# A gated sum of a long convolution and a GLU: one table for the last stage of the inverse transform, fewer warming matmuls, two down products in another bank, and new queue orders

## The chip, the core and the metric

The kernel runs on one core of a Trainium2 chip. The core has five engines, each with its own instruction queue that is worked off in order: TensorE (PE, with its weight loads shown apart as PEld), VectorE (DVE), ScalarE (ACT), GpSimd (POOL) and SyncE (SP), which only issues DMAs. The metric is the device time of one execution in microseconds (us), lower is better. Comparisons are of medians of several runs on one chip.

## The reference, cut to what matters

```python
x = A_u                                            # (1, 2048, 448), f32
g = sigmoid((x * gate_w).sum(-1, keepdims=True))   # one gate per position
# branch a: a diagonal state-space convolution over the 2048 positions
A = -exp(log_A_real) + 1j * A_imag                 # (448, 256)
C = (C_real + 1j * C_imag) * dt[:, None]
K = 2 * einsum("dn,dnl->dl", C, exp((A * dt[:, None])[:, :, None] * pos)).real
y = irfft(rfft(K, 4096) * rfft(u.T, 4096), 4096)[:, :2048]
a = y.T + u * D_skip
# branch b: GLU with a sigmoid gate, 448 -> 1792 -> 448
b = (sigmoid(x @ w_gate) * (x @ w_up)) @ w_down
out = g * a + (1 - g) * b
```

Both branches read the same x (an input B_x is drawn but not used).

## The kernel before, in words

**Four pieces of work.** (1) *Prologue* (`step_sizes`, `params`, lines 998 to 1176): from the small parameters come the step sizes, phases and powers of the convolution kernel, mostly on VectorE and ScalarE. `step_sizes` also holds the warming: `WAKE` matmuls of a tile of ones into a PSUM tile that nobody reads (L1030), first in TensorE's queue. `params` broadcasts the step sizes over the partitions with one matmul (L1072) whose input is two scaled identity blocks made on VectorE (L1069).

(2) *Kernel generation* (`kgen`, 28 chunks of 16 channels): GpSimd makes powers (`powers`), TensorE multiplies positions by phases (L1223) and subtracts the whole turns (L1232), ScalarE rounds and takes sines (L1227 to L1245; L1229 makes the whole turns that L1232 needs), VectorE forms outer products (L1252) and multiplies them in (L1266, L1269), TensorE contracts (L1281, after the second half chunk's L1269), and ScalarE copies the result to `ke` (L1302). After chunk 13 and chunk 27 a half of the channels is complete: VectorE adds the skip weights to `ke` (L1306) and the half goes to DRAM.

(3) *Transforms* (class `Chain`): a transform of 4096 points as two stages of table matmuls, for u (two halves of the channels) and for K (two halves, called chains 0 and 1 here). For each K half: `stage1` (L812), a transposition, `product` with the spectrum of u (L845, L879, L889), a transposition, and `back`: the last stage of the inverse, 16 blocks j, each two matmuls (L926) with a quarter q = j // 4 of the table `t1t`, then one VectorE instruction (L930) that scales by the gate and adds to the output tile.

(4) *GLU* (`glu_groups`): for each half H of the positions and each group of the 14 feature blocks, `glu_up` (L1414 to L1419, rounded f32 in three products, gate L1398, L1400 or L1403 to L1406) and `glu_down` (L1433 in plain f32 or L1435 to L1437 in three rounded products), with L1445 or L1452 taking the result from PSUM into the output tile `ob`.

**Memory.** PSUM tiles come from pools by tag: `gu` has two, `dn` one, `fps` of pool fups two, of pool fkps three. In `back` each chain loads the four quarters of `t1t` itself, 256 KB each, into a tile with tag `ft` (chain 1, two buffers) or `ftx` (chain 0, which has moved to pool fk by then; one buffer), so a load waits until the tile before it has been used.

**What sets the order.** Instructions are first only recorded (`Plan.op`). The table `PLACE` gives each of them its place in its engine's queue, by engine, tag and priority; it was written by a search outside this file. `Plan.order` merges the queues with a cost model of the engines and emits them. The places within an engine are fixed by the table: an instruction that has to wait holds up all that is behind it on its engine, SyncE's DMA issues too.

The two lines that name the numbers that change:

```python
SX = {'ft': 1, 'ua': 2, 'fps': 2}
WAKE = 24
```

Of the kernel before, what the change touches and what calls it, by code (L numbers as in the profile page):

```python
# [20 lines left out]
HD = 224  # L21
# [7 lines left out]
    ('Act', 'aci', 10): (15, 36,),  # L29
    ('Act', 'aci', 19): (64, 87,),  # L30
    ('Act', 'acr', 10): (13, 34, 43,),
    ('Act', 'acr', 19): (60, 85, 94,),
# [26 lines left out]
    ('Act', 'dots', 1): (27,),  # L59
    ('Act', 'dots', 2): (50,),  # L60
    ('Act', 'dots', 16): (80, 82,),
# [284 lines left out]
SX = {'ft': 1, 'ua': 2, 'fps': 2}  # L346
# [352 lines left out]
WAKE = 24  # L699
# [879 lines left out]
```

## Time and profile before

| | |
|---|---|
| median of 3 runs | 691.46 us (689.62 to 694.54) |
| span of the profiled execution | 688.4 us |
| its own time | not given apart; the median is 3.1 us above the span, the lowest run 1.2 |
| TensorE busy | 673.8 us |
| VectorE busy | 602.0 us |
| ScalarE busy | 510.0 us |
| DMA | 123.84 MB, 180 GB/s on average |

The page gives the busy time of each engine, the span in 40 slices of 17.2 us, the chain of work that ended last, and groups of instructions by line with the tiles that they write and read. Names like `dn_gps` are tag and pool. An idle time is shown with what ended it, `<-` and the instruction. The starts of matmuls tell more than their durations, since matmuls overlap.

### The profile page before, as it was taken

Reading aid. Unit: us, or ns where it says so; the run is one execution under the profiler, and the core shown is the slowest. Engines: PE = TensorE matmul, PEld = TensorE weight load, DVE = VectorE, ACT = ScalarE, POOL = GpSimd, SP = SyncE. Lnnn points to the kernel's source line nnn. Section 1 sums busy time; section 2 is a strip of 40 time slices with the busy share of each in tenths; the row PEclk is TensorE's granted clock in tenths of the full one; section 3 lists DMA queues with packets and bytes.
Section 4 is the critical chain, followed back from the end, with each engine's and each line's share of the span. In section 5 each row is a group of like instructions: output and inputs, shape, how many; then the busy total and the mean of one; then the engine's idle time right before and its main releaser. Section 6 shows DMA issues by size and latency. Waiting matters only on the chain.

```text
span 688.4 us, 16283 instructions
## 1 busy us (share of the span) xinstructions
PE 673.8 (98%) x6588; PEld 483.1 (70%) x6588; DVE 602.0 (87%) x699; ACT 510.0 (74%) x928; POOL 274.9 (40%) x280
## 2 busy tenths in 40 slices
PE   9999999999999999999899999999999999999996
PEld 8776667877886687775556676788888766556873
DVE  5999999999999999989999789999973489577976
ACT  5677699899999999999999999999941352233110
POOL 0315268865447656675663845667000000000000
PEclk9999999999999999999999999999999999999999
DMA  9769342656896787737966974457948973979866
GB/s 252 180 177 246 87 108 70 153 138 237 186 182 157 177 215 178 225 112 177 193 171 144 233 199 90 140 168 184 180 100 202 271 235 124 312 246 241 166 179 165
DMA packets 97474, 123.84 MB, mean 180 GB/s; under 512 B 31096, under 2 KB 80568, under 8 KB 96376
## 3 DMA queue, kind: packets, MB, share of 16 engines
q1 hardware_dynamic: 97400, 122.81, 69.8%
q8 instruction: 52, 0.85, 0.5%
q14 instruction: 22, 0.18, 0.1%
HBM read 79.20 MB, written 43.58 MB: 178 GB/s over the span
## 4 chain that ended last, share of the span: by engine, by line
PE 73%; ACT 10%; DVE 8%; DMA 5%; issue 2%; SPq 1%; ACTq 0%; DVEq 0%
PE gu_gps L1414 9%; PE gu_gps L1415 8%; PE gu_gps L1416 8%; PE kp_egp L1281 6%; PE dn_gps L1433 5%; PE dn_gps L1435 4%; PE tp_egp L1232 4%; PE dn_gps L1436 4%; PE dn_gps L1437 4%; PE tp_egp L1223 4%; PE fps_fups L812 3%; PE gu_gps L1418 3%; PE gu_gps L1419 3%; PE fps_fups L845 2%; PE fps_fups L889 2%
## 5 line engine op out<-in xcount | busy, mean ns | idle before, releaser
L1414 PE MATMUL gu_gps<-xs_glu,wh_glu 128*128 128x512 f32 x336 | 144.5, 430 | 1.4 <-DVE hl_glu L1400 0.9
L1416 PE MATMUL gu_gps<-xs_glu,wl_glu 128*128 128x512 f32 x336 | 131.8, 392 | 0.0
L1415 PE MATMUL gu_gps<-xs_glu,wh_glu 128*128 128x512 f32 x336 | 131.7, 392 | 0.0
L1269 DVE TENSOR_TENSOR cs_eg<-cs_eg,es_eg 128x2048 f32<-128x2048 f32 x56 | 129.2, 2307 | 1.4
L1252 DVE TENSOR_TENSOR es_eg<-tb_eg 128x1024 f32<-128x1024 f32 x112 | 110.5, 1003 | 3.0 <-POOL tb_eg L1216 0.9
L1213 POOL TENSOR_TENSOR tb_eg<-tb_eg 128x96 f32<-128x96 f32 (+2 forms) x84 | 107.5, 1284 | 5.9
L1216 POOL TENSOR_TENSOR tb_eg<-tb_eg,bs_eg 128x32 f32<-128x32 f32 x84 | 83.9, 1001 | 5.8
L1414 PEld LDWEIGHTS gu_gps<-xs_glu,wh_glu 128*128 128x128 f32 x336 | 63.2, 188 | 30.2 <-issue 13.0
L1398 ACT ACTIVATE sg_glu<-gu_gps 128x512 f32<-128x512 f32 x56 | 33.7, 603 | 58.3 <-PE gu_gps L1419 58.3
L1266 DVE TENSOR_TENSOR cs_eg<-cs_eg,es_eg 128x1024 f32<-128x1024 f32 x56 | 70.5, 1260 | 7.2 <-ACT cs_eg L1245 6.0
L1229 ACT ACTIVATE nn_eg<-cs_eg 128x512 fp32r<-128x512 f32 x112 | 71.7, 640 | 4.5 <-PE tp_egp L1232 2.9
L1415 PEld LDWEIGHTS gu_gps<-xs_glu,wh_glu 128*128 128x128 f32 x336 | 63.3, 188 | 15.4 <-issue 4.8
L1416 PEld LDWEIGHTS gu_gps<-xs_glu,wl_glu 128*128 128x128 f32 x336 | 63.1, 188 | 14.5
L1452 DVE SCALAR_TENSOR_TENSOR ob_glu<-dn_gps,og,ob_glu 128x448 f32<-128x448 f32 x72 | 48.7, 676 | 25.1 <-PE dn_gps L1437 24.1
L1234 ACT ACTIVATE cs_eg<-tp_egp 128x512 f32<-128x512 f32 x112 | 66.5, 605 | 4.1 <-PE tp_egp L1232 3.6
L1227 ACT ACTIVATE cs_eg<-tp_egp 128x512 f32<-128x512 f32 x112 | 67.9, 607 | 1.6 <-PE kp_egp L1281 0.6
L1235 ACT ACTIVATE cs_eg<-tp_egp 128x512 f32<-128x512 f32 x112 | 67.3, 606 | 1.6 <-PE tp_egp L1232 1.4
L1245 ACT ACTIVATE cs_eg<-cs_eg,half_pi 128x1024 f32<-128x1024 f32 x56 | 65.2, 1165 | 0.4
L1281 PEld LDWEIGHTS kp_egp<-cs_eg 128*32 128x32 f32 x3584 | 51.5, 110 | 11.7 <-issue 6.3
L1281 PE MATMUL kp_egp<-cs_eg 128*32 128x64 f32 x3584 | 56.3, 220 | 0.5 <-issue 0.4
L1203 POOL MEMSET tb_eg<- 128x96 f32 x28 | 7.8, 285 | 116.4 <-DVE es_eg L1252 105.5
L1232 PE MATMUL tp_egp<-nn_eg,idn 128*128 128x512 f32 x112 | 49.7, 444 | 3.9 <-ACT nn_eg L1229 3.4
(161 smaller groups left out, 1326.2 us busy)
## 6 DMA issues: line engine op xcount, KB each, us to landing
shf<-fx_fu SPq DMA_DIRECT2D x16, 896.0 KB
fx_fu<-shf SPq DMA_DIRECT2D x16, 896.0 KB
us<-fx_fu SPq DMA_DIRECT2D x16, 896.0 KB
xr_glu<-in_w_dram SPq DMA_DIRECT2D x46, 256.0 KB
uax_fk<-us SPq DMA_DIRECT2D x16, 448.0 KB
ua_fk<-us SPq DMA_DIRECT2D x16, 448.0 KB
xr_glu<-in_w_dram SPq DMA_DIRECT2D x17, 224.0 KB
gt_pre<-in_u_dram SPq DMA_DIRECT2D x8, 448.0 KB
```

Of the source, the lines that this page charges most:

```text
L1213: pool(96 * m, lambda n=n, m=m: G.tensor_mul(g3(n + 1, m), g3(1, m), g3(n, 1).to_broadcast([128, 32, 3, m])))
L1216: pool(32, lambda e=e: G.tensor_mul(t(e + 1), t(e), b(3)))
L1227: op("Act", c_act(512, True), lambda: S.activation(cs[:, 1, ds, 32:96], block(tp), AF.Copy, bias=MAGIC), [tp], [(cs, ("s", i))], prio)
L1229: op("Act", c_act(512), lambda: S.activation(block(nn), cs[:, 1, ds, 32:96], AF.Copy, scale=-1.0, bias=MAGIC), [(cs, ("s", i))], [nn], prio)
L1232: op("PE", c_mm(532), lambda: T.matmul(tp.real, idn.real, nn.real, start=False, stop=True, skip_group_check=True), [nn, idn], [tp], prio)
L1252: V.tensor_mul(o.rearrange("p d (i k) -> p d i k", k=ny), x.unsqueeze(3).to_broadcast([128, 16, nx, ny]), y.unsqueeze(2).to_broadcast([128 ...
L1266: op("DVE", c_dve(1024), lambda: V.tensor_mul(cs[:, :, :, 0:32], cs[:, ::-1, :, 63:31:-1], es[:, :, 0:32].unsqueeze(1).to_broadcast([128, ...
L1269: op("DVE", c_dve(2048), lambda: V.tensor_mul(cs[:, :, :, 32:96], cs[:, :, :, 32:96], es[:, :, 32:96].unsqueeze(1).to_broadcast([128, 2, 1 ...
L1281: T.matmul(kp[32 * j:32 * j + 32, q], cs[:, z, 4 * j + q, 64:96], cs[:, z, 4 * j + q, 0:64], start=cs is parts[0] and z == 0 and q == 0, s ...
L1414: T.matmul(p.real, wh[:, k, cs], x[:, k], start=(k == 0), stop=False)
L1415: T.matmul(p.real, wh[:, k, cs], x[:, 4 + k], start=False, stop=False)
L1416: T.matmul(p.real, wl[:, k, cs], x[:, k], start=False, stop=False)
```

## The change

- `back` takes its table from one tile `t1` of all four quarters (8 KB in each partition, pool fk), loaded once by whichever chain asks first, quarter by quarter; both chains read it. The tags `ftx` and the last four uses of `ft` in chain 1 are gone. Eight loads become four.
- `WAKE` is 14 instead of 24.
- In the last GLU group of the second half, the down products of j = 5 and j = 7 use a `gu` tile of PSUM in place of the one `dn` tile.
- `PLACE` is a new table for all five engines. It has the same instructions apart from these.

The diff, without the table:

```diff
-SX = {'ft': 1, 'ua': 2, 'fps': 2}
+SX = {'ua': 2, 'fps': 2}
...
-WAKE = 24
+WAKE = 14
...
             hs = slice(self.h * HD, (self.h + 1) * HD)
-            tb = self.tile("ft", (128, TN, 128))
-            dma(lambda: tb.v("p l c -> p (l c)"), lambda: t1t[:, 512 * q:512 * q + 512], 128 * 2048,
-                [], [tb], prio)
+            tb = back_table(q, prio)
             for i in range(4 * q, 4 * q + 4, 2):
                 self.back_pair(i, tb, hs)
...
-                    T.matmul(p[64 * i:64 * i + 64, :HD], tb[:, l // 2, 64 * (l % 2):64 * (l % 2) + 64], x[:, 2 * j + i],
+                    T.matmul(p[64 * i:64 * i + 64, :HD], tb[:, j // 4, l // 2, 64 * (l % 2):64 * (l % 2) + 64], x[:, 2 * j + i],
                              start=True, stop=True)
             op("PE", c_mm4(HD, 2, COLS), f,
-               [tb, (x, j), *([] if self.on_dve else [(x, ("t", i)) for i in range(4)])], [p], self.prio)
+               [(tb, j // 4), (x, j), *([] if self.on_dve else [(x, ("t", i)) for i in range(4)])], [p], self.prio)
...
-    xs, ob = {}, {}
+    def back_table(q, prio):
+
+        if "t1" not in tables:
+            tables["t1"] = fk.tile("t1", 1, (128, 4, TN, 128))
+        t1 = tables["t1"]
+        if q not in tables:
+            tables[q] = True
+            dma(lambda: t1[:, q].rearrange("p l c -> p (l c)"), lambda: t1t[:, 512 * q:512 * q + 512], 128 * 2048,
+                [], [(t1, q)], prio)
+        return t1
+
+    xs, ob, tables = {}, {}, {}
...
     def glu_down(H, fs, j, hs, first, pe, prio):
-        p = gps.tile("dn", 1, (128, 512))
+        end = H == 1 and fs == FGS[1][-1] and j in (5, 7)
+        p = gps.tile("gu", GUB, (128, 512)) if end else gps.tile("dn", 1, (128, 512))
```

Of the table, three entries in full, the places of the broadcast L1072 (first number) with its two followers, of L1306, and of the loads of the last-stage table (old: the last four of the first line and the second line; the first four of it belong to `stage1`):

```diff
-    ('PE', 'fps', 10): (20, 56, 57,),
+    ('PE', 'fps', 10): (14, 55, 56,),
-    ('DVE', 'ke', 20): (348, 514,),
+    ('DVE', 'ke', 20): (350, 517,),
-    ('SP', 'ft', 41): (261, 272, 280, 284, 289, 292, 337, 351,),
-    ('SP', 'ftx', 40): (276, 333, 345, 354,),
+    ('SP', 'ft', 41): (266, 278, 284, 287,),
+    ('SP', 't1', 40): (264, 295, 277, 281,),
```

What these places mean where the prediction uses them, read out of the two tables:

```
VectorE near L1306 of the first half
  old: L1266, L1269 (chunk 13), L1306, L1252, L1345, L1252, L1266, L1452, L1400 (hl), L1269 (chunk 14)
  new: L1266, L1269 (chunk 13), L1452, L1252, L1400 (hl), L1306, L1252, xs, xs, L1452, L1266, L1269 (chunk 14)
TensorE at the start, matmuls ahead of L1072 and after the warming: old 53, new 36
TensorE work between L1223 and L1232 of a turn, shortest three of 112: old 0.2, 0.9, 1.0 us; new 1.4 us and up
TensorE, inverse blocks (L926) in a row, in the order of the runs:
  old 8, 6, 10, 2, 2, 2, 2      new 12, 6, 4, 3, 3, 3, 1
TensorE, the last eight: old  dn j4, L926, L926, dn j5, L926, L926, dn j6, dn j7
                         new  dn j4, dn j5, L926, L926, L926, dn j6, L926, dn j7
TensorE, groups of plain f32 products after the warming: old 72, new 69
TensorE, other changes of the array's shape: old 172, new 174
```

More of the change, by code (lines that the diff above doesn't have):

```diff
@@ L28 @@
 PLACE = {
[L29 to L32, printed above, removed]
[26 rows of a table removed]
[L59 to L61 removed]
[18 rows of a table removed]
[L80 to L82 removed]
[12 rows of a table removed]
[L95 removed]
[13 rows of a table removed]
+    ('Act', 'aci', 10): (14, 40,),
+    ('Act', 'aci', 19): (65, 94,),
+    ('Act', 'acr', 10): (15, 39, 49,),
+    ('Act', 'acr', 19): (63, 91, 101,),
[26 rows of a table added]
+    ('Act', 'dots', 1): (28,),
+    ('Act', 'dots', 2): (45,),
+    ('Act', 'dots', 16): (67, 83,),
[18 rows of a table added]
+    ('Act', 'idn', 10): (12,),
+    ('Act', 'junk', 10): (29, 60,),
+    ('Act', 'junk', 19): (77, 81, 132,),
[12 rows of a table added]
+    ('Act', 'pos_sb', 10): (36, 52,),
[13 rows of a table added]
     ('Act', 'wh', 0): (1, 4,),
     ('Act', 'wh', 1): (6, 7,),
[4 rows of a table removed]
[4 rows of a table added]
     ('Act', 'xs', 0): (0, 2, 3, 5,),
[2 rows of a table removed]
[L118 to L121 removed]
[15 rows of a table removed]
[L137 to L138 removed]
[14 rows of a table removed]
[L153 removed]
[24 rows of a table removed]
[L178 to L180 removed]
[6 rows of a table removed]
[L187 removed]
[6 rows of a table removed]
[L194 removed]
[71 rows of a table removed]
[2 rows of a table added]
+    ('DVE', 'aci', 10): (45,),
+    ('DVE', 'aci', 19): (122,),
+    ('DVE', 'acr', 10): (89,),
+    ('DVE', 'acr', 19): (152,),
[15 rows of a table added]
+    ('DVE', 'dtp', 10): (30,),
+    ('DVE', 'dtv', 10): (27,),
[14 rows of a table added]
+    ('DVE', 'half_pi', 0): (9,),
[24 rows of a table added]
+    ('DVE', 'ones', 10): (1,),
+    ('DVE', 'p', 10): (18, 20, 21, 22, 23, 25, 26,),
+    ('DVE', 'phs', 20): (2,),
[6 rows of a table added]
+    ('DVE', 'skip', 20): (0,),
[6 rows of a table added]
+    ('DVE', 'uax', 40): (539, 534, 546, 547, 556, 557, 570, 571, 578, 575, 585, 586, 590, 591, 595, 596, 624, 623,
[71 rows of a table added]
     ('Pool', 'bsx1', 10): (5, 11,),
[3 rows of a table removed]
[3 rows of a table added]
         56, 57, 58, 59, 60, 61, 62, 63, 64, 65, 66, 67, 68, 69, 70, 71, 72, 73, 74, 75, 76, 77, 78, 79, 80, 81, 82,
```

16 lines of the change are left out of this document (removed), and 530 rows, old and new, of the table PLACE.

## The prediction

> **What bounds the kernel now.** I read the page first: span, engines, slices, chain.
>
> ```profile
> span 688.4 us, 16283 instructions
> PE 673.8 (98%) x6588; PEld 483.1 (70%) x6588; DVE 602.0 (87%) x699; ACT 510.0 (74%) x928; POOL 274.9 (40%) x280
> ...
> DVE  5999999999999999989999789999973489577976
> ...
> PE 73%; ACT 10%; DVE 8%; DMA 5%; issue 2%; SPq 1%; ACTq 0%; DVEq 0%
> ```
>
> TensorE is busy for 98% of the span and carries 73% of the chain; VectorE is nearly as full until 500 us, while the convolution kernel is generated. A saving must be less work on TensorE or less idling there, and the idling is only 688.4 - 673.8 = 14.6 us. The waits of TensorE, and its busy time in some windows, say where.
>
> ```profile
> PE tp_egp L1232 <- ACT nn_eg L1229: 3.4, 7, 0.9
> ...
> PE dn_gps L1435 <- DVE ob_glu L1452: 0.8, 1, 0.8
> PE fps_fups L926 <- DMA ftx_fk<-in_t1t_dram: 0.6, 1, 0.6
> ```
>
> ```profile
> 684.00:689.00 5.00, 0.00 (x0) 0.73 0.44 104
> 310.00:350.00 40.00, 35.64 (x486) 1.00 0.87 172
> ```
>
> The columns of a window are its length, the busy time with the instructions, granted clock, DMA share and GB/s. TensorE idles 4.4 us between 310 and 350, from before 684 to the end, and 1.1 us at the start (the row of L1030 below). The code change touches the start and the waits of 0.6 and 0.8; only the new queue orders can touch the 4.4.
>
> A run's time is the span and what lies around it: the median of the three runs, 691.46, is 3.1 above this span, the lowest, 689.62, is 1.2 above. I work out differences for the profiled execution and put them on the median. The three runs differ by 0.7%, so less than about 1%, 6.9 us, can't be told from no change.
>
> **The start: 14 warming matmuls instead of 24.**
>
> ```profile
> L1030 PE MATMUL fps_fups<-ones_pro 112*128 112x128 f32 x48 | 8.5, 362 | 1.1 <-DVE half_pi L1497 1.1
> ```
>
> ```profile
> 2.05:3.05 1.00, 1.00 (x7) 1.00 0.94 307
> ...
> 7.50:8.50 1.00, 1.00 (x12) 1.00 0.99 355
> ```
>
> ```profile
> 6.54 0.69 DVE L1345 TENSOR_TENSOR xs_glu<-xr_pre,xs_glu 128x512 fp32r<-128x512 f32 x1 [0.51 <-ACT xs_glu L1341]
> ...
> 9.29 0.48 PE L1414 MATMUL gu_gps<-xs_glu,wh_glu 128*128 128x512 f32 x1
> ...
> 9.55 0.42 DVE L1347 TENSOR_TENSOR xs_glu<-xr_pre,xs_glu 128x256 fp32r<-128x256 f32 x1
> ...
> 10.46 0.69 DVE L1381 TENSOR_TENSOR wl_glu<-xr_pre,wh_glu 128x512 fp32r<-128x512 f32 x1
> ...
> 11.07 0.17 DVE L984 TENSOR_SCALAR xr_pro<-x_pro 112x4 f32<-112x4 f32 x1
> ...
> 11.27 0.17 DVE L984 TENSOR_SCALAR x_pro<-x_pro 112x4 f32<-112x4 f32 x1
> ...
> 20.22 0.27 DVE L1069 TENSOR_SCALAR rt_pro<-idn,dtv_pro 112x112 f32<-112x112 f32 x1
> ...
> 21.41 0.54 PE L1072 MATMUL fps_fups<-rt_pro,ones_pro 112*128 112x224 f32 x2
> ```
>
> A matmul of L1030 is two records. A window counts every record that overlaps it, so 7 records of about 0.4 us in 1 us are 5 starts per us. Fourteen matmuls, all in this slow part, take 28 / 5 = 5.6 us and end near 6.9. The first real matmuls need the L1345 that ends at 7.2, so TensorE starts them 2.0 us earlier. It can't keep that. After nine matmuls it needs the second part of x, which the L1347/L1348 pair from 9.55 to 10.46 makes; the new VectorE order puts a small step (0.2, from 11.07 to 11.27) and a one-column memset (0.1) in front of the pair, so 10.76. The old queue runs 53 matmuls from 9.29 to 21.41, 0.229 each, and starts the tenth at 11.35. Gained so far: 0.6.
>
> Then the new queue gives it back. L1072, which broadcasts the step sizes, now comes after 36 matmuls, not 53, so TensorE asks for it at 10.76 + 27 x 0.229 = 16.9. Its input is the second L1069. By the new order VectorE has from 9.55 until that is done two pairs of L1347/L1348 (0.91), four steps of 512 columns (0.61, from 10.46 to 11.07), twenty small ones (0.20) and the memset: 1.82 + 2.44 + 4.0 + 0.1 = 8.4, so 17.9. TensorE waits 1.0 us, and the 17 matmuls that used to come first stand behind: they end at 17.9 + 0.22 + 3.9 = 22.0, where the old queue is at 21.6. I take +0.4. Without that wait it is -0.6; with the input as late as now, at 20.5, it is +3.0.
>
> The granted clock is given as 1.00 in both windows above, yet the starts go from 5 to some 9 per us (12 records of about 0.3 us). The Trainium skill ("TensorE: Matmul & The Clock Gate", Part 1) says that the array runs at half rate until a free-running window of about 3.4 us has been busy, and again after an idle one. The slow part here, over 5 us, agrees. By that rule shortening the warming could leave real matmuls in the slow part; that is rival 4.
>
> **The end: the table and the bank.**
>
> ```profile
> 672.81 0.55 SPq L712 DMA_DIRECT2D ftx_fk<-in_t1t_dram  x1
> ...
> 675.31 5.15 SPq L712 DMA_DIRECT2D out_dram<-ob_glu  x8
> ...
> 676.83 0.98 PE L926 MATMUL fps_fups<-fx_fu,ftx_fk 128*64 128x224 f32 x8 [0.57 <-DMA ftx_fk<-in_t1t_dram]
> ...
> 681.17 4.44 SPq L712 DMA_DIRECT2D out_dram<-ob_glu  x7
> ...
> 682.78 0.47 PE L1435 MATMUL dn_gps<-vh_glu,hh_glu 128*128 128x448 f32 x1 [0.78 <-DVE ob_glu L1452]
> ...
> 683.68 0.69 DVE L1452 SCALAR_TENSOR_TENSOR ob_glu<-dn_gps,og,ob_glu 128x448 f32<-128x448 f32 x1 [0.96 <-PE dn_gps L1437]
> ```
>
> Eight loads of table quarters become four, all placed in SyncE's queue in the product stage. Of the old eight, three were there too, so that stage gets one issue more (0.55, hidden by SyncE's own waits; without that cover the input load behind it is 0.55 later), and the last 35 us lose five. The wait of 0.57 goes, since no quarter's buffer has to come free. The last down product no longer waits 0.78 for VectorE to empty the one dn bank. Together -1.35.
>
> What is late next? VectorE and the stores. Seven stores follow each other without a gap, 0.63 each, and the last two come right behind the last L1452, which ends at 684.37. Moved 1.35 forward they would meet a queue that is still busy, but two table loads (0.55 and about the same) leave that queue, which covers most of it. VectorE is nearer:
>
> ```profile
> L930 DVE SCALAR_TENSOR_TENSOR ua_fk<-fps_fkps,gs,ua_fk 128x224 f32<-128x224 f32 x8 | 3.6, 444 | 0.1
> ```
>
> ```profile
> 653.64 0.76 PE fps_fkps L926 x8
> ```
>
> (The second row is of the chain: eight records are two blocks, 0.38 each.) The new TensorE order starts with twelve inverse blocks in a row where there were eight, with five PSUM tiles between TensorE and VectorE, and VectorE needs 0.44 for each and has a vl step of 0.64 among them. That order makes TensorE wait about 12 x 0.06 = 0.7. So -0.65 in all; the ends are 0 and -1.35.
>
> **The middle: the orders.**
>
> ```profile
> 302.51 2.29 DVE L1269 TENSOR_TENSOR cs_eg<-cs_eg,es_eg 128x2048 f32<-128x2048 f32 x1
> 307.80 0.22 DVE L1306 TENSOR_TENSOR ke_eg<-ke_eg,skip 128x56 f32<-128x56 f32 x1 [2.99 <-ACT ke_eg L1302]
> 307.94 1.22 DVE L1252 TENSOR_TENSOR es_eg<-tb_eg 128x1024 f32<-128x1024 f32 x1
> 309.07 0.68 DVE L1345 TENSOR_TENSOR xs_glu<-xr_glu,xs_glu 128x512 fp32r<-128x512 f32 x1
> ...
> 312.00 0.67 DVE L1400 SCALAR_TENSOR_TENSOR hl_glu<-sg_glu,gu_gps 128x512 f32<-128x512 f32 x1
> 312.60 2.28 DVE L1269 TENSOR_TENSOR cs_eg<-cs_eg,es_eg 128x2048 f32<-128x2048 f32 x1
> ```
>
> At the end of the first half L1306 needs the contraction that itself needs the L1269 just before it, so VectorE stands for 2.99 us. The new order puts an L1452, an L1252 and an L1400 between the two: 0.6 + 1.13 + 0.6 = 2.3 us of work that VectorE has to do anyway. And VectorE is what the next 40 us wait for:
>
> ```profile
> 330.00:340.00 10.00, 7.76 (x146) 4.76 (x145) 9.86 (x8) 9.04 (x17) 7.83 (x7) 1.00 1.16 191
> ```
>
> ```profile
> 331.14 0.50 PE L1232 MATMUL tp_egp<-nn_eg,idn 128*128 128x512 f32 x1 [0.89 <-ACT nn_eg L1229]
> ...
> 339.28 0.50 PE L1232 MATMUL tp_egp<-nn_eg,idn 128*128 128x512 f32 x1 [0.78 <-ACT nn_eg L1229]
> ```
>
> (The first row: TensorE, its weight loads, VectorE, ScalarE, GpSimd.) The two waits of L1232 lie where the old order has only 0.2 to 1.0 us of other TensorE work between L1223 and L1232 of a turn (chunk 16); in the new order the shortest such distance is 1.4. These waits and VectorE's 2.3 lie in the same 4.4 us and can't be added. I take -3.0, nearer to the 4.4 than to the 0 that it is if ScalarE, 90% busy in the row above, sets the pace.
>
> ```profile
> 28.14 0.74 PE L1418 MATMUL gu_gps<-xs_glu,wh_glu 128*128 128x512 f32 x1
> 28.72 0.40 PE L1419 MATMUL gu_gps<-xs_glu,wl_glu 128*128 128x512 f32 x1
> ```
>
> The first rounded matmul after a plain f32 group takes 0.58 to the next one, not 0.23. The old order has 72 such groups, the new 69: -1.05. Other changes of the array's shape go from 172 to 174: +0 to +0.7, at the same price. I take -0.7. All other work is the same instructions in nearly the same places; I give it 0, with 2 us either way.
>
> **Sum.** +0.4 - 0.65 - 3.0 - 0.7 = -3.95, so 691.46 - 3.95 = 687.5.
>
> **Rivals.** 1. The gains are hidden: ScalarE paces the middle, VectorE and the stores the end. For it speaks ScalarE's 9.04 and VectorE's 9.86 of 10 us above. 691.46 + 0.4 - 0.7 = 691.2.
>
> 2. All of it comes: -4.4, -1.35, -0.6 and -1.05 are -7.4, 684.1. For it: the waits are plain in the rows. Against: something is always late next in a kernel that is this full.
>
> 3. Slower: ScalarE's queue holds the turns. Between L1227 and L1229 of a turn the new order has on average 0.37 more foreign ScalarE instructions than the old.
>
> ```profile
> L1229 ACT ACTIVATE nn_eg<-cs_eg 128x512 fp32r<-128x512 f32 x112 | 71.7, 640 | 4.5 <-PE tp_egp L1232 2.9
> ```
>
> At 0.64 that is 0.24 us per turn. On the 28 turns whose matmuls stand less than 2.5 us of TensorE work apart it becomes a TensorE wait of 6.6 us in all, and the gain of the middle is lost: 691.46 + 0.4 - 0.65 - 0.7 + 6.6 = 697.1. It decides where ScalarE is already late when L1227 is ready. Against it: the shortest distances grow.
>
> 4. The clock. TensorE idles some 1.4 us before 10.8 and 1.0 before 17.9. If that brings the slow rate back for as long as it lasted at the start, 5.6 us, 5/9 of the work is done in that time and the rest is late: 5.6 x 4/9 = +2.5, so 690.0. For it: the start is slow for that long at the same shown clock of 1.00. Against it: no stretch after the start shows the slow rate, but none before 310 idles as much either. The Trainium skill's page named above asks for a whole idle window before the rate falls, more than either gap; by that rule rival 4 doesn't come.
>
> **How the numbers follow.** The forecast has 0.46, rival 1 0.23, rival 2 0.18, rival 3 0.08, rival 4 0.05. The range leaves out most of rival 3 and the better half of rival 2: 683.0 to 694.0; the upper end is rival 1 with the late input at the start (3.0 instead of 0.4). The forecast's own range is 685 to 690. Faster by over 1% (under 684.5): two thirds of rival 2 and a tenth of the forecast, 0.18 with rounding up. Slower by over 1% (over 698.4): a third of rival 3 and what I haven't thought of, 0.06. Within: 0.76.
>
> **What would show it.** In the profile after: L1030 with 28 records ending before 7.3 and a wait of about 1 us at L1072 near 17 (right) or none (-0.6); L1306's first wait under 1 us and TensorE busy for over 38 of the 40 us from 310 (right), or VectorE's idle time moved elsewhere and TensorE's as before (rival 1); no wait for a table and none at the last down product; L1232's waits under 2 us in all, or over 6 (rival 3). I'm wrong if the time is under 683 without these, or if a new wait of several us stands in TensorE's list.

## The result, and the profile after

The changed kernel takes 688.62 us (median of 20 runs, 684.96 to 693.69) beside 692.16 us of the kernel before (20 runs, 689.62 to 695.45) on the same chip: a ratio of 0.9945, 95% interval 0.9924 to 0.9965, so 2.4 to 5.3 us less. On the 691.46 us of the prediction that is 687.7, where 687.5 was forecast. The sum was right. Its terms were not all right, and one cause that can move the time by more than any of them, late code for TensorE, was not in it.

The profiled execution took 684.96 us. The span, the engines, VectorE's slices and the chain of waits of its page:

```profile
span 683.0 us, 16235 instructions
...
PE 669.7 (98%) x6568; PEld 480.6 (70%) x6568; DVE 603.7 (88%) x699; ACT 509.7 (75%) x928; POOL 269.2 (39%) x280
...
DVE  7998999999899999999998999999974379667976
...
PE 82%; DVE 10%; ACT 3%; DMA 2%; issue 2%; SPq 1%; DVEq 0%
```

TensorE now carries 82% of the chain where it carried 73%; ScalarE's share fell from 10% to 3%. TensorE's busy time fell by 4.1 us and its idle time, 683.0 - 669.7 = 13.3 us, by 1.3. Line numbers from about 1039 on are nine or ten higher than before (L1315 is L1306, L1241 is L1232, L1462 is L1452).

The list of TensorE's waits (total, times, longest):

```profile
PE dn_gps L1443 <- DVE ob_glu L1462: 1.3, 2, 0.8
PE tp_egp L1241 <- ACT nn_eg L1238: 1.2, 1, 1.2
...
PE dn_gps L1445 <- DVE ob_glu L1462: 1.0, 1, 1.0
...
PE gu_gps L1423 <- DVE hh_glu L1409: 0.6, 1, 0.6
PE dn_gps L1443 <- DMA vh_glu<-in_w_dram: 0.5, 1, 0.5
PE fps_fups L1081 <- DVE rt_pro L1078: 0.4, 1, 0.4
```

The 3.4 us of L1232 are 1.2, and neither the wait for the table (0.6) nor that of the last down product (0.8) is in the list any more. The 1.0 of L1445 is another wait for the one dn bank, at 659.9, in the stretch of the inverse: VectorE empties the bank late there, after it has stood 0.86 us for a load (L928 at 658.45). Most of what is new stands in the head of the kernel: the timeline of TensorE there.

```profile
6.81 0.48 PE L1423 MATMUL gu_gps<-xs_glu,wh_glu 128*128 128x512 f32 x1
...
16.09 0.65 PE L1081 MATMUL fps_fups<-rt_pro,ones_pro 112*128 112x224 f32 x2 [0.41 <-DVE rt_pro L1078]
...
29.32 1.02 PE L1443 MATMUL dn_gps<-vh_glu,hl_glu 128*128 128x448 f32 x2 [0.45 <-DMA vh_glu<-in_w_dram]
...
30.95 0.50 PE L1423 MATMUL gu_gps<-xs_glu,wh_glu 128*128 128x512 f32 x1 [0.61 <-DVE hh_glu L1409]
...
34.11 1.02 PE L1443 MATMUL dn_gps<-vh_glu,hh_glu 128*128 128x448 f32 x2 [1.05 <-ACT ob_glu L1455]
```

The first real matmul is 2.5 us earlier than before (9.29), the broadcast of the step sizes 5.3 us earlier (21.41). Then three waits of 2.1 us in all follow within 5 us.

The end of the first half on VectorE, and TensorE's window behind it:

```profile
302.44 2.35 DVE L1278 TENSOR_TENSOR cs_eg<-cs_eg,es_eg 128x2048 f32<-128x2048 f32 x1
304.70 0.67 DVE L1462 SCALAR_TENSOR_TENSOR ob_glu<-dn_gps,og,ob_glu 128x448 f32<-128x448 f32 x1
305.30 1.21 DVE L1261 TENSOR_TENSOR es_eg<-tb_eg 128x1024 f32<-128x1024 f32 x1
306.43 0.67 DVE L1409 SCALAR_TENSOR_TENSOR hl_glu<-sg_glu,gu_gps 128x512 f32<-128x512 f32 x1
307.86 0.22 DVE L1315 TENSOR_TENSOR ke_eg<-ke_eg,skip 128x56 f32<-128x56 f32 x1 [0.75 <-ACT ke_eg L1311]
```

```profile
310.00:350.00 40.00, 37.85 (x506) 24.42 (x506) 39.40 (x36) 37.94 (x69) 28.11 (x27) 1.00 0.91 186
```

The wait of 2.99 is 0.75, and TensorE is busy 37.85 of the 40 us instead of 35.64, with 20 more matmuls.

To see where the time went in this and the other runs, each span is cut at five instructions: the first matmul of the contraction (L1281) of chunks 0, 13, 20 and 27, and of the first inverse block (L926). The kernels of the experiments are explained below; all numbers are us from one profile each.

| kernel | to chunk 0 | 0 to 13 | 13 to 20 | 20 to 27 | to inverse | to end | span |
|---|---|---|---|---|---|---|---|
| before | 114.9 | 190.0 | 97.8 | 102.0 | 146.4 | 37.2 | 688.4 |
| before, L1306 later | 113.7 | 190.8 | 97.8 | 103.4 | 146.3 | 38.1 | 690.0 |
| before, and sine earlier | 113.8 | 190.8 | 97.7 | 103.0 | 146.3 | 37.4 | 689.0 |
| before, table and bank | 113.3 | 189.8 | 97.8 | 103.1 | 146.3 | 36.8 | 687.1 |
| before, 14 and 10 short | 113.5 | 190.2 | 97.8 | 104.6 | 146.3 | 37.2 | 689.6 |
| before, 22 and 8 short | 114.7 | 190.6 | 98.2 | 102.0 | 146.3 | 37.1 | 688.9 |
| before, 14 warming | 113.7 | 196.5 | 97.6 | 106.8 | 146.4 | 37.8 | 698.7 |
| after | 115.1 | 190.0 | 95.3 | 102.2 | 144.6 | 35.9 | 683.0 |
| after, second profile | 117.5 | 194.0 | 95.2 | 102.1 | 144.6 | 35.7 | 689.1 |
| after, 24 warming | 115.2 | 191.6 | 96.7 | 102.2 | 146.1 | 35.1 | 686.8 |
| after, 12 and 8 short | 115.7 | 190.6 | 96.0 | 102.4 | 145.8 | 35.7 | 686.2 |
| after, that and L1315 back | 114.1 | 190.5 | 97.5 | 102.4 | 146.1 | 36.0 | 686.5 |
| after, L1315 back | 114.1 | 193.4 | 97.4 | 101.9 | 144.6 | 35.1 | 686.4 |
| after, 4 and 53 short | 134.8 | 205.9 | 103.1 | 107.9 | 144.6 | 34.7 | 731.1 |

From before to after the profiles give +0.2, 0.0, -2.5, +0.2, -1.8, -1.4: -5.4 with rounding. The work in the columns is not quite the same. To chunk 0 the new kernel has three GLU matmuls less and one phase matmul more (0.5 us less work), from 0 to 13 three GLU matmuls more (0.7 us), from 13 to 20 five more and one phase matmul less (4 x 0.23 = 0.9 us), from 20 to 27 two more (0.5 us), and between chunk 27 and the inverse seven less (1.6 us). So the true gains are some 3.4 us behind the end of the first half, 1.4 us at the end, 0.7 and 0.3 us in the columns from 0 to 13 and from 20 to 27, and between chunk 27 and the inverse next to nothing. To chunk 0 something is lost: the first real matmul is 2.5 us earlier, there is less work, and yet the kernel gets there no earlier.

Three variants of the changed kernel (24 warming; 12 and 8 short, with and without L1315 back) are 1.2 to 1.5 us slower than the others between chunk 27 and the inverse. All of this arises in one group of L889 near 620 us. In front of it VectorE's L879 (L771 in the variants) waits for a load of `uax`, 2.6 to 2.7 us in the four other profiles and 4.2 to 4.6 in these three (two of the three name a matmul that ended just then as what ended the wait, the other profiles the load). TensorE's group behind it takes 3.2 us in the four and 4.3 to 4.6 in the three. VectorE's rows of the changed kernel and of that with 12 and 8 short:

```profile
613.87 2.08 DVE L879 TENSOR_TENSOR uax_fk<-uax_fk,fps_fups 128x896 f32<-128x896 f32 x2 [2.59 <-DMA uax_fk<-us]
```

```profile
617.65 2.08 DVE L771 TENSOR_TENSOR uax_fk<-uax_fk,fps_fups 128x896 f32<-128x896 f32 x2 [4.18 <-DMA uax_fk<-us]
```

The load was issued 104.2 us behind the start of chunk 27's contraction in both. Why it lands later in the second stays open.

The times spread, by 8.7 us for the changed kernel: its profiled execution is one of its quickest, and its gain by spans (5.4) is more than by medians (3.5). The second profile, of 690.99 us, shows two events that make such a difference, below.

### The profile page after: what moved, and what is told of

The parts are those of the page before. It is cut to its first block, busy times and chain, and to the rows that moved or that the text cites. A ratio compares the mean times of both kernels' runs of the same rounds, so it can differ in the third digit from the quotient of the medians.

```text
span 683.0 us, 16235 instructions
## 1 busy us (share of the span) xinstructions
PE 669.7 (98%) x6568; PEld 480.6 (70%) x6568; DVE 603.7 (88%) x699; ACT 509.7 (75%) x928; POOL 269.2 (39%) x280
## 4 chain that ended last, share of the span: by engine, by line
PE 82%; DVE 10%; ACT 3%; DMA 2%; issue 2%; SPq 1%; DVEq 0%
PE gu_gps L1423 10%; PE gu_gps L1424 9%; PE gu_gps L1425 9%; PE kp_egp L1290 7%; PE dn_gps L1443 6%; PE dn_gps L1445 5%; PE tp_egp L1232 4%; PE tp_egp L1241 4%; PE dn_gps L1446 4%; PE dn_gps L1447 4%; PE fps_fups L812 3%; PE gu_gps L1427 3%; PE fps_fups L845 3%; PE gu_gps L1428 3%; PE fps_fups L889 2%; PE fps_fkps L889 2%
## 5 line engine op out<-in xcount | busy, mean ns | idle before, releaser
L1423 PE MATMUL gu_gps<-xs_glu,wh_glu 128*128 128x512 f32 x336 | 144.6, 430 | 1.6 <-DVE hl_glu L1409 0.8
L1278 DVE TENSOR_TENSOR cs_eg<-cs_eg,es_eg 128x2048 f32<-128x2048 f32 x56 | 131.5, 2349 | 1.4
L1222 POOL TENSOR_TENSOR tb_eg<-tb_eg 128x96 f32<-128x96 f32 (+2 forms) x84 | 118.8, 1416 | 6.1
L1238 ACT ACTIVATE nn_eg<-cs_eg 128x512 fp32r<-128x512 f32 x112 | 74.9, 669 | 3.8 <-PE tp_egp L1241 2.6
L1243 ACT ACTIVATE cs_eg<-tp_egp 128x512 f32<-128x512 f32 x112 | 70.0, 636 | 3.1 <-PE tp_egp L1241 2.7
L1236 ACT ACTIVATE cs_eg<-tp_egp 128x512 f32<-128x512 f32 x112 | 69.9, 633 | 2.7 <-PE tp_egp L1232 1.0
L1244 ACT ACTIVATE cs_eg<-tp_egp 128x512 f32<-128x512 f32 x112 | 69.0, 627 | 1.1 <-PE tp_egp L1241 1.1
L1254 ACT ACTIVATE cs_eg<-cs_eg,half_pi 128x1024 f32<-128x1024 f32 x56 | 66.7, 1191 | 0.2
L1225 POOL TENSOR_TENSOR tb_eg<-tb_eg,bs_eg 128x32 f32<-128x32 f32 x84 | 62.6, 745 | 6.4
L1462 DVE SCALAR_TENSOR_TENSOR ob_glu<-dn_gps,og,ob_glu 128x448 f32<-128x448 f32 x70 | 47.4, 677 | 16.0 <-PE dn_gps L1447 15.1
L1241 PE MATMUL tp_egp<-nn_eg,idn 128*128 128x512 f32 x112 | 51.4, 459 | 1.2 <-ACT nn_eg L1238 1.2
```

The costliest lines, as they stand in the source:

```text
L1222: pool(96 * m, lambda n=n, m=m: G.tensor_mul(g3(n + 1, m), g3(1, m), g3(n, 1).to_broadcast([128, 32, 3, m])))
L1236: op("Act", c_act(512, True), lambda: S.activation(cs[:, 1, ds, 32:96], block(tp), AF.Copy, bias=MAGIC), [tp], [(cs, ("s", i))], prio)
L1238: op("Act", c_act(512), lambda: S.activation(block(nn), cs[:, 1, ds, 32:96], AF.Copy, scale=-1.0, bias=MAGIC), [(cs, ("s", i))], [nn], prio)
L1241: op("PE", c_mm(532), lambda: T.matmul(tp.real, idn.real, nn.real, start=False, stop=True, skip_group_check=True), [nn, idn], [tp], prio)
L1243: op("Act", c_act(512, True), lambda: S.activation(cs[:, 0, ds, 32:96], block(tp), AF.Abs), [tp], [(cs, ("c", i))], prio)
L1278: op("DVE", c_dve(2048), lambda: V.tensor_mul(cs[:, :, :, 32:96], cs[:, :, :, 32:96], es[:, :, 32:96].unsqueeze(1).to_broadcast([128, 2, 1 ...
```

## The experiments

The kernels of the experiments write the table of places on fewer lines, so their line numbers are 108 lower than those of before or after (99 lower against before where the table's loading is put in, 106 against after and before with the short warming matmuls).

**Moving L1306 alone.** VectorE's queue of before, at the end of the first half:

```diff
 L1269  chunk 13
-L1306  first half
 L1252
 L1345
 L1252
+L1306  first half
 L1266  chunk 14
```

> The kernel before with one instruction moved: the first L1306 stands three VectorE instructions later (behind an L1252, an L1345 and another L1252, 2.3 to 2.9 us of work). Theory (VectorE's wait of 2.99 us at the end of the first half is what the next 40 us pay for): L1306 waits under 1 us, TensorE is busy over 37.5 of the 40 us from 310 where it was 35.64, and the time is 2.2 to 3.0 us under the kernel before, ratio 0.9957 to 0.9968. Rival (ScalarE paces the middle, VectorE's wait is hidden): the wait shrinks, but TensorE's busy time there stays under 36.5, the contractions of chunks 16 to 20 start where they did, and the ratio is 0.999 to 1.001.

Measured: 692.66 us, ratio 1.0019 (1.0001 to 1.0037). VectorE's queue of this kernel:

```profile
307.77 0.21 DVE L1198 TENSOR_TENSOR ke_eg<-ke_eg,skip 128x56 f32<-128x56 f32 x1
309.65 1.23 DVE L1158 TENSOR_TENSOR cs_eg<-cs_eg,es_eg 128x1024 f32<-128x1024 f32 x1 [1.67 <-ACT cs_eg L1137]
```

```profile
310.00:350.00 40.00, 35.62 (x488) 22.68 (x491) 39.15 (x35) 37.58 (x67) 25.51 (x23) 1.00 0.88 172
```

The wait at L1306 is gone (0.21 is its own time), but L1266 (here L1158) then waits 1.67 us for the sine L1245, which ScalarE works off no earlier than before. TensorE is busy 35.62 us of the 40, as before, and the stretch from 13 to 20 is 97.8 in both. The rival holds for the old orders: the wait was real and hidden. (The time is even a little up. The profile has a stall of 1.12 us near 479, in the column from 20 to 27; see below.)

**And the sine earlier.** In ScalarE's queue the two copies L815 in front of that sine go behind the next L1229.

```diff
 L1235
-L815
-L815
 L1245  second sine of chunk 14
 L1227
 L1398
 L1229
+L815
+L815
```

> The kernel before with the first L1306 three VectorE instructions later, as in the earlier run, and with two L815 copies of ScalarE's queue moved from in front of the sine L1245 to behind the next L1229. Theory (with the wait at L1306 covered, ScalarE's order was late next: the sine that VectorE then waited 1.67 us for, and the L1229 that TensorE waits 0.81 for near 311): VectorE's wait before L1266 near 309 falls from 1.67 to under 0.8, TensorE's wait near 311 falls from 0.81 to about 0, and the contractions from chunk 15 on start 0.7 to 1.0 us earlier than with L1306 moved alone; ratio to the kernel before 0.998 to 1.000. Rival (the middle is bound by VectorE's work and the moves only shift waits): chunks 16 to 20 start within 0.3 us of where they do with L1306 moved alone.

Measured: 691.37 us, ratio 1.0002 (0.9988 to 1.0015). VectorE, then TensorE:

```profile
308.89 1.28 DVE L1158 TENSOR_TENSOR cs_eg<-cs_eg,es_eg 128x1024 f32<-128x1024 f32 x1 [0.81 <-ACT cs_eg L1137]
```

```profile
312.41 0.50 PE L1124 MATMUL tp_egp<-nn_eg,idn 128*128 128x512 f32 x1 [0.82 <-ACT nn_eg L1121]
```

VectorE's wait fell from 1.67 to 0.81 as the theory has it, but TensorE waits as long as it did, one turn later, it is busy 35.71 us of the 40, and the stretch is 97.7. One more repair only moved the wait to ScalarE's next turn. So by these two runs the old orders hold TensorE at several places at once here.

**Moving it back in the new orders.** The changed kernel, with L1315 again directly behind chunk 13's L1278 (the reverse of the first diff).

> The changed kernel with one instruction moved back: the first L1315 (L1306 of before) stands directly behind the L1278 of chunk 13, as in the kernel before. Theory (the cover at the end of the first half carries the gain of the middle): VectorE waits about 3 us there, TensorE's busy time from 310 to 350 falls from 37.85 to about 35.5, and the time is 2.2 to 3.0 us over the changed kernel, so 0.9977 to 0.9989 of the kernel before. Rival (the gain comes from the distances in TensorE's and ScalarE's orders): the wait is back, but the contractions of chunks 16 to 20 start within 0.7 us of where they do in the changed kernel, and the ratio to the kernel before stays at 0.994 to 0.995.

Measured: 690.79 us, ratio 0.9981 (0.9959 to 1.0002), so some 2.5 us over the changed kernel. TensorE was busy 36.76 us of the 40, not the 35.5 that the theory foretold. Its profile had a TensorE stall of 2.44 us at 254 as well, ahead of the place in question, so the move was made once more on the kernel with 12 and 8 short ones, which comes below:

> The changed kernel with the first L1315 back directly behind the L1278 of chunk 13, and with the 12 and 8 warming matmuls whose stream length did well: the earlier run of this move had a stall for code near 254 us in its trace. Theory (the cover of that wait carries part of the middle in the new orders): VectorE waits about 3 us, the contraction of chunk 15 is 1.5 to 2.5 us later than in the kernel with the same warming and the move not made, ratio 0.9945 to 0.997 where that kernel had 0.9925. Rival (the 2.5 us of the earlier run were the stall): ratio 0.992 to 0.9935.

Measured: 688.84 us, ratio 0.9961 (0.9940 to 0.9982), beside 0.9925 without the move.

```profile
307.34 0.22 DVE L1209 TENSOR_TENSOR ke_eg<-ke_eg,skip 128x56 f32<-128x56 f32 x1 [3.10 <-ACT ke_eg L1205]
```

The wait is back (3.10), and the stretch from 13 to 20 is 97.5 instead of 96.0; chunk 15's contraction is 1.7 us later against it. So the same move is worth 1.5 to 2.5 us in the new orders and nothing in the old ones.

**The table and the bank alone.** The orders of before; the table as in the change, loaded at four of the old places; the last down products j = 5 and 7 in `gu`.

```diff
-            tb = self.tile("ft", (128, TN, 128))
+            tb = back_table(q, prio)
...
-        p = gps.tile("dn", 1, (128, 512))
+        end = H == 1 and fs == FGS[1][-1] and j in (5, 7)
+        p = gps.tile("gu", GUB, (128, 512)) if end else gps.tile("dn", 1, (128, 512))
```

> The kernel before with the table of the last stage in its own tile, loaded once by four transfers at the old places in SyncE's queue, and with the two last down products in the other bank; all orders else as they were, 24 warming matmuls. Theory (both waits at the end were the end's own): the wait of 0.57 for the table and that of 0.78 for the last down product are gone, nothing is late next, the stretch from the first inverse block to the last matmul is 1.35 us shorter, ratio 0.998. Theory of the forecast (half of it is taken back): 0.65 us, ratio 0.999. Rival (VectorE and the stores pace the end): the waits move to other rows and the stretch is as long as it was, ratio 1.000.

Measured: 690.07 us, ratio 0.9981 (0.9966 to 0.9995): -1.3 us. Both waits are gone and the last matmul starts at 680.66, 2.6 us earlier than in the profile of before, of which 0.8 was there at the first inverse block already. But the span is only 1.2 us shorter. SyncE's queue shows why:

```profile
679.36 0.62 SPq L604 DMA_DIRECT2D out_dram<-uax_fk  x1
680.03 4.49 SPq L604 DMA_DIRECT2D out_dram<-ob_glu  x7
```

The last seven stores still follow each other without a gap; they end at 684.5, 1.1 us earlier than before (681.17 + 4.44), and the kernel ends 2.6 us behind them, as it did before (2.8). The stretch from the first inverse block to the end is 36.8 instead of 37.2, so this profile shows 0.4 us of gain in the end itself, where the last matmul came 1.8 us earlier against the first inverse block. The times say 1.3, but with an interval of 0.3 to 2.4 they can't tell 0.4 from 1.35. In the new orders the stretch is 34.7 to 36.0.

**Fourteen warming matmuls alone.**

```diff
-WAKE = 24
+WAKE = 14
```

> The kernel before with 14 warming matmuls in place of 24, and all its orders as they were. Theory (the warming only covers the load of the first inputs, and what it frees is taken back before the first contraction, at 115 us): the first real matmul starts near 6.8 instead of 9.29, L1072 waits 2 to 4 us for its VectorE input near 18 to 20, the first contraction starts within 0.7 us of 115, and the ratio is 0.999 to 1.001. Rival (the start goes straight into the time): the first contraction is 1.5 to 2.5 us earlier, ratio 0.9965 to 0.9978. Rival of the clock (the idle time brings the slow rate back): the first contraction is 1.5 to 3 us later, ratio 1.002 to 1.004.

Measured: 701.28 us, ratio 1.0138 (1.0110 to 1.0166): 9.5 us slower, which no theory had. The first contraction came at 113.7, like in the other profiles with 24. The loss lies far behind it. TensorE's timeline:

```profile
187.62 0.79 PE L1311 MATMUL gu_gps<-xs_glu,wl_glu 128*128 128x512 f32 x1 [3.68 <-issue]
...
490.46 0.79 PE L1307 MATMUL gu_gps<-xs_glu,wh_glu 128*128 128x512 f32 x1 [2.68 <-issue]
```

```profile
184.00:185.00 1.00, 0.00 (x0) 0.00 (x0) 1.00 (x1) 0.60 (x1) 0.00 (x0) 1.00 1.21 220
...
187.00:188.00 1.00, 0.38 (x1) 0.38 (x2) 0.45 (x1) 0.00 (x0) 0.00 (x0) 0.50 1.16 189
190.00:191.00 1.00, 1.00 (x4) 0.80 (x3) 0.00 (x0) 0.87 (x3) 0.00 (x0) 0.50 1.20 164
...
194.00:195.00 1.00, 1.00 (x6) 0.84 (x5) 1.00 (x2) 0.41 (x1) 0.00 (x0) 1.00 1.18 217
```

TensorE stands for 3.68 us and waits for nothing that the profile shows ("issue"); then its granted clock is 0.50 for 6.8 us. VectorE and ScalarE run dry behind it. A second such stall, of 2.68 us, ends at 490, with 3.4 us at 0.50 behind it. The DMA share is 1.16 to 1.21 in these rows. The DMA queues of the stall (packets, MB, share), and those of the whole run of before:

```profile
q1 hardware_dynamic: 815, 0.72, 113.1%
q8 instruction: 1, 0.02, 2.3%
```

```profile
q8 instruction: 52, 0.85, 0.5%
```

Fifty-two packets of queue 8 are 0.85 MB, 16 KB each. TensorE's records in that run are 13,354 (6588 loads, 6588 matmuls, 178 others): 257 for each packet. So TensorE's code comes in blocks of 256 instructions while the kernel runs. In the 14 profiles of this study 27 gaps of over 0.25 us on TensorE are without a releaser (23) or end 0.25 us or more after the one named (4), where other waits end within 0.1. Every one of them stands at the same place of TensorE's stream, 193 to 195 instructions behind a multiple of 256, and ends 1.2 to 1.6 us after such a packet has landed. So that place is where TensorE has used up its code. The earliest packets start some 270 to 290 instructions ahead of it, so no request seems to come sooner. That is 32 us of GLU matmuls (140 x 0.23), but 5 us when a contraction (256 instructions in 1.9 us) lies between. And in a DMA burst the packet starts late: the one at 184.7 landed at 186.0, 7 us after TensorE had come to the mark of 280. Ten matmuls less at the start are 40 instructions less, and every block then ends 40 instructions elsewhere.

**The same short start with the stream's old length.**

```diff
-WAKE = 24
+WAKE, PAD = 14, 10
...
+            for _ in range(PAD):
+                T.matmul(wake[:, :8], ones.real, ones.real[:, :8], start=True, stop=True)
```

> The kernel before with 14 warming matmuls of 128 columns and ten more of 8 columns: the start is as short as with 14, but TensorE's instruction stream is as long as with 24. Theory (the 10 us that 14 warming matmuls alone cost come from where TensorE's 16 KB blocks of code end: two of them were fetched late, behind a burst of DMA packets): TensorE's two stalls without a releaser (3.68 us near 184, 2.68 near 488) and the halved clock behind them are gone, the first contraction is about 1 us earlier than 115.1, and the time is 0 to 1.5 us under the kernel before, ratio 0.998 to 1.000. Rival (the shorter start itself does it, by clock or timing): the stalls stay and the ratio stays near 1.014.

Measured: 693.75 us, ratio 1.0039 (1.0021 to 1.0058). The stall at 184 and the slow clock are gone, and with them some 7 of the 9.5 us. Not the rest: a stall of 1.88 us stays at 480, in a contraction. This profile, of 691.36 us, is of the quickest of the twelve executions of this kernel; what the others lose beyond it is in no trace, but their mean granted clock is on record, and it falls with their time, from 0.998 at 691.36 to 0.993 at 697.11. Three of the four other profiles of the old orders at this length have a stall near 480 too (0.33 to 1.12 us; in the column from 20 to 27 they lose 1.0 to 1.4 us against before). Before's own profile has none there, and was a lucky one in this.

**Other lengths.** Three more kernels differ from before or after only in the warming.

```diff
+WAKE, PAD = 22, 8      # before's orders, 24 instructions more
+WAKE, PAD = 12, 8      # after's orders, 24 instructions more
+WAKE, PAD = 4, 53      # after's orders, 172 instructions more
```

> The kernel before with 22 warming matmuls of 128 columns and eight of 8 columns: TensorE's stream is 24 instructions longer, all else as it was. Theory of the code blocks: in the traces of the old orders the fetch near 477 us comes late in four of five executions (the contraction there lost 0.6 to 2.2 us); this length moves the block's end away from it, so the time is 1 to 2 us under the kernel before, ratio 0.997 to 0.9985, and no stall without a releaser stands near 480. Rival (the length of the stream matters only in rare cases): ratio 0.9995 to 1.001.

Measured: 691.25 us, ratio 0.9989 (0.9969 to 1.0010). The column from 20 to 27 is 102.0, so the stall near 480 is gone, but three of about half a microsecond stand at 210, 349 and 391. Undecided between the two theories by time.

> The changed kernel with 12 warming matmuls of 128 columns and eight of 8 columns: the start no longer than with 14, TensorE's stream 24 instructions longer. Theory (the changed kernel's times, 684.96 to 693.69, spread because a block of code is fetched late in some executions; this length leaves most time for each fetch by its trace): median 684.5 to 687, ratio 0.990 to 0.993, and the spread is smaller. Rival (the spread has another cause): median 688 to 689, ratio 0.994 to 0.996, the same spread.

Measured: 686.32 us (686.16 to 688.37), ratio 0.9925 (0.9909 to 0.9941). One stall stands in the profile, 0.56 us at 309; the list of waits puts it down to ScalarE, which had ended 0.5 us before. By the ratios this is the quickest version of the study, some 1.4 us under the changed kernel, but the intervals overlap, so that it is better is not shown. Its six times lie within 2.2 us, as foretold; twelve of the same length with L1315 moved back spread over 5.5 us.

> The changed kernel with 4 warming matmuls of 128 columns and 53 of 8 columns: TensorE's stream is 172 instructions longer than with 14, which by the changed kernel's trace puts the requests for new code just ahead of the contractions inside DMA bursts. The start is some 2 to 3 us later, of which little should reach the first contraction. Theory of the code blocks: stalls of TensorE without a releaser of 1.5 to 4 us near 490 and near 250, perhaps smaller ones near 190 and 220, with the halved clock after the longest, so 5 to 12 us over the changed kernel, ratio 1.001 to 1.012. Rival (only the start matters): no such stalls, 0 to 2 us over it, ratio 0.9945 to 0.9975.

Measured: 732.40 us, ratio 1.0583. Two things came out otherwise. The start took 20 us more, not 2 to 3:

```profile
3.04 22.62 PE L933 MATMUL fps_fups<-ones_pro 112*128 112x8 f32 x106
...
29.93 0.63 PE L1318 MATMUL gu_gps<-xs_glu,wh_glu 128*128 128x512 f32 x1
...
31.10 0.40 PE L1317 MATMUL gu_gps<-xs_glu,wh_glu 128*128 128x512 f32 x1
```

The 8-column matmuls start 0.21 apart through all 22.6 us, as slowly as the first of 128 columns, and only after 5 us of real matmuls the rate rises (0.63 to 0.40). In the kernels with 8 or 10 short ones, which run behind the rise of the clock, they start 0.11 apart. And there were six stalls for code of 2.4 to 5.1 us, 20.9 in all, with slow clock behind five of them; between the first contraction and the last the kernel lost 29.5 us. So the stream's length matters as the theory says, but most places were not those foretold (220, 255, 291, 360, 435, 539 instead of 490 and 250, with smaller ones at 190 and 220). With the start off by 20 us, the bursts probably lay elsewhere against the code.

**24 warming matmuls in the changed kernel.**

> The changed kernel with 24 warming matmuls. Theory of the forecast (the start's 2.5 us are taken back before the first contraction): first real matmul near 8 to 9.3, first contraction within 0.7 us of 115, the same time as the changed kernel, 0.993 to 0.996 of the kernel before. Theory of the code blocks (40 more instructions in TensorE's stream put the block ends elsewhere): a stall without a releaser can appear or go; from the places of the contractions and DMA bursts in the changed kernel's trace this shift leaves the requests less exposed at 179, 305 and 475 us and more at 265, so no loss over 3 us. Rival (the shorter warming is what gains): 1.5 to 2.5 us slower than the changed kernel, ratio 0.997 to 0.999.

Measured: 690.39 us, ratio 0.9984 (0.9967 to 1.0002), some 2.7 us over the changed kernel. To chunk 0 it is 115.2 against 115.1, as the forecast has it: the start is worth nothing. The rest is not the same: 1.6 us are lost from chunk 0 to 13 (0.46 of it a wait for a load at 141, the rest in small pieces), 1.4 from 13 to 20, where TensorE stands 2.37 us for code at 350, and 1.5 between chunk 27 and the inverse, with the late load told above.

**The changed kernel once more.**

> The changed kernel as it is, once more beside the next two. Expected by every theory: median 687.5 to 689.5, ratio 0.992 to 0.997. Theory of the code blocks: some of its executions have a late fetch and a fall of the clock, so its times spread over 5 us or more. Rival: no such spread beside the other kernels here.

Measured: 688.09 us (684.30 to 692.37), ratio 0.9943 (0.9916 to 0.9970). This time the profiled execution was a long one, 690.99 us. Its list of waits begins

```profile
PE dn_gps L1335 <- DMA vh_glu<-in_w_dram: 2.7, 1, 2.7
PE kp_egp L1182 <- issue: 2.6, 1, 2.6
```

The wait of 0.45 at 29 us for the down weights is 2.74 here, with a clock of 0.50 for 3.4 us behind it, and TensorE stands 2.58 us for code at 258. Against the first profile this one is 2.4 us later at chunk 0, 1.0 more (in small pieces) at chunk 2 and 2.9 more at chunk 10; from there on the difference stays between 6.3 and 6.5. So these two events make 5.3 of it. The other executions have no trace, so that their spread comes from the like is not shown. What is on record of them fits: of the 32 of the changed kernel the twelve under 687 us had a mean granted clock of 0.998 to 1.000, the eight over 690 us one of 0.994 to 0.998.

## Why the prediction was right, and where it was not

**The sum.** -3.95 was forecast, -3.8 came out by the ratio. By the columns, the head gave +0.2 for +0.4, 13 to 20 gave -2.5 for -3.0, the end -1.4 for -0.65, and the other three -1.6 together, where -0.7 was forecast for fewer plain groups and 0 for the rest. So much of the agreement is luck of terms.

**The start** (+0.4). The warming ended as worked out: 28 records in 6.9, measured 7.05. The wait at L1072 is 0.41, not 1.0, at 16.09, not 17.9. The failed step is "twenty small ones (0.20)". VectorE's timeline in the changed kernel:

```profile
10.47 0.16 DVE L996 SCALAR_TENSOR_TENSOR f_pro<-k_pro,x_pro 112x4 f32<-112x4 f32 x1
10.66 0.17 DVE L996 SCALAR_TENSOR_TENSOR f_pro<-k_pro,f_pro 112x4 f32<-112x4 f32 x1
10.74 0.69 DVE L1390 TENSOR_TENSOR wl_glu<-xr_pre,wh_glu 128x512 fp32r<-128x512 f32 x1
11.35 0.16 DVE L993 TENSOR_SCALAR k_pro<-k_pro 112x4 f32<-112x4 f32 x1
11.42 0.16 DVE L993 TENSOR_SCALAR p_pro<-f_pro 112x4 f32<-112x4 f32 x1
...
15.57 0.47 DVE L1078 TENSOR_SCALAR rt_pro<-idn,dtv_pro 112x112 f32<-112x112 f32 x2
```

A small step holds the queue for 0.20 only where the next one needs its result (10.47 to 10.66); otherwise the next starts 0.07 to 0.08 later (10.66 to 10.74, 11.35 to 11.42). So VectorE needed 7.1 us from 8.95 until both L1069 were done, at 16.04, and not 8.4. At 21 us the kernel was 1.2 us ahead, not 0.4 behind. It didn't help. The prediction stopped looking at 22 us, and the new order waits 2.1 us from 29 to 34; at 37 us the kernel was 1.0 behind. At the first contraction after stands at 115.1, before at 114.9, and the other profiles of the old orders at 113.3 to 114.7, those of the new at 114.1 to 117.5 (without the one with the long start). By the two profiles the term is +0.2, by the means of seven and six +1.4, for another reason than the one given.

**The middle** (-3.0). Right in size: -2.5 between chunks 13 and 20, with 0.9 us more work done there. The step "VectorE is what the next 40 us wait for" was half of it. In the old orders covering VectorE's wait gives nothing, since ScalarE's sine is late next; that was the mechanism of the rival in which ScalarE paces the middle. The cover gives 1.5 to 2.5 us only together with the rest of the new orders. That it is their wider spacing of a turn's steps that makes the difference is likely, but no run took ScalarE's and TensorE's orders apart. That the waits of L1232 and VectorE's "can't be added" was right, and for a stronger reason: in the old orders each hides behind the other. The bound set for TensorE's window (over 38 of 40) was missed by 0.15.

**The end** (-0.65). The stretch from the first inverse block to the end is 1.4 us shorter, so for the whole change the term was too small. For the part that was reasoned about, the table and the bank, its size may be right: alone they took 0.4 us off the stretch in their profile, and 1.3 (0.3 to 2.4) off the time. That something is taken back came true; the reason given failed. TensorE's wait of 0.7 in a row of inverse blocks doesn't exist. In the list of groups of the changed kernel the idle time before them is 0.0 (L924 is L926 of before):

```profile
L924 PE MATMUL fps_fups<-fx_fu,t_fk 128*64 128x224 f32 x64 | 8.3, 359 | 0.0
L924 PE MATMUL fps_fkps<-fx_fk,t_fk 128*64 128x224 f32 x64 | 8.2, 357 | 0.0
```

What was late next in the run of the table and the bank was the other candidate named, the stores. The new orders took some more from there (34.7 to 36.0 to the end, beside 36.8), by what, no run took apart.

**Fewer plain groups** (-0.7). No run took them apart; it stays open.

**All other work** (0, with 2 us either way). This is the step that failed most. "The same instructions in nearly the same places" is not nothing where the length of TensorE's stream changes: in the old orders the same edit, 24 to 14, cost 9.5 us, and 7 of them went away with the old length alone. The new orders had the luck to be exposed less at their length: their first profile has no such stall, their second one of 2.58 us. The blocks of code were on the page of before (queue 8, 52 packets), and the prediction passed over them.

**The rivals.** ScalarE's queue holding the turns did not come: L1232's waits fell to 1.2. The clock did not fall back in the first 22 us; the only wait behind the first real matmul there, 0.41, was far shorter than those that made it fall. It did fall at 29 us in the second profile, behind the wait of 2.74 for the down weights, which the rival did not name. The rival in which the gains are hidden was right in its mechanisms where parts were tried alone (ScalarE in the middle, the stores at the end), and wrong for the whole.

## What to carry to other kernels

In a kernel of this length count the code as a transfer with a due time: find the instruction queue in the list of DMA queues, divide the engine's instructions by its packets, and look where a stretch of many short instructions meets a DMA burst. An edit that only changes how many instructions stand ahead of that place can then cost more than what it saves, and a change of a few dummy instructions is a cheap thing to try. And a wait that is plain in one engine's row is worth what it stands for only if no other engine is late at the same place: cover it alone, and see, before adding it to a sum.

## What the runs showed of the hardware

- **Late code.** TensorE stops 193 to 195 instructions behind a multiple of 256 when the next 16 KB block has not landed; 27 of 27 gaps of that kind in 14 profiles stood there, and each ended 1.2 to 1.6 us after the block's landing. The stops were 0.3 to 5.1 us long.
- **The clock can fall after less than 3 us.** It went to 0.50 behind waits of TensorE of 2.37, 2.54, 2.68, 2.74 and 3.48 to 5.09 us, and did not behind others of 2.37, 2.44, 2.58 and 3.27. The slow stretches lasted 3.41 or 6.83 us by the clock's records in the trace. The Trainium skill ("TensorE: Matmul & The Clock Gate", Part 1) tells of a free-running window of 3.4 us, which fits the lengths. It also asks for a whole idle window before the rate falls, as the prediction cited it for rival 4; here it fell behind an idle time of 2.37 us, and the measurement decides.
- **Narrow matmuls did not warm.** Behind 4 warming matmuls of 128 columns and 53 of 8 the clock had not risen after 24 us of unbroken matmuls (one kernel; its six executions, 731.0 to 735.1 us, were all long). In the other 13 profiles it rose 3.2 to 6.0 us after the first warming matmul of 128 columns, so that behind the same 24 matmuls the first real one started anywhere from 8.06 to 9.29.
